# DeltaNet and multiplicative FFN on one core: the first two chunks' keys and queries transposed on TensorE, four buffers for float64 pieces, w3 and w_out loaded from ScalarE's queue, the FFN listed one chunk later

## The chip, the core and the metric

The kernel runs on one core of one Trainium2 chip. The core has five engines, each of which works through its own list of instructions in order: TensorE (PE, with its weight loads shown apart as PEld), VectorE (DVE), ScalarE (ACT), GpSimd (POOL) and SyncE (SP). SP only issues DMAs here; ACT can issue them as well. The metric is the device time of one execution in microseconds (us). A measurement of this kernel can tell a change of about 1% from no change.

## The reference

```python
def _attn_ref(q, k, v, beta):            # each (4, 8, 768, 48); beta (4, 8, 768)
    k_n = k / (np.linalg.norm(k, axis=-1, keepdims=True) + 1e-06)
    state = np.zeros((B, H, D, D))
    for t in range(S):
        kt, vt, bt = k_n[:, :, t], v[:, :, t], beta[:, :, t, None]
        y[:, :, t] = np.einsum('bhd,bhde->bhe', q[:, :, t], state)
        v_old = np.einsum('bhde,bhd->bhe', state, kt)
        state = state + bt[..., None] * np.einsum('bhd,bhe->bhde', kt, vt - v_old)

def _moe_ref(x, w1, w2, w3, w_out):      # x (3072, 384); w1, w2 (384, 1024)
    a = x @ w1                           # w3 (1024, 1024); w_out (1024, 384)
    b = x @ w2
    h = a * b @ w3
    return h @ w_out
```

The output of the first part, reordered to 3072 tokens by 384 features, is the input x of the second. The four FFN weights come as float64; q, k, v and beta as float32.

## The kernel before, in words

**Chunks.** The 768 tokens are cut into 12 chunks of 64. For one chunk all 4 batches and 8 heads are worked on together: r is the pair of batches, z the batch in it, and z picks the upper or lower half of the 128 partitions. Inside a chunk the recurrence is written as matrix products with a triangular inverse.

**What one chunk needs.** `load_tok` loads keys by token (tile `ktok`, three buffers) and `load_v` values (`vtok`). `load_perm` loads keys and queries once more, in 32x32 blocks, into the zero-padded tiles `kperm` and `qperm`: 16 small DMAs for each r, that is 32 for a chunk. `prep` turns them with DVE's 32x32 transposes into `KQ` (features on partitions, L201), multiplies keys with keys and queries on PE (L205, the "scores"), and writes `U` and `PT` on DVE (L212, L216). `norms(j)` computes the key norms of two chunks. `to_blocks`, `inverse` and `from_blocks` send U through DRAM (`Ud`), read it back as 32x32 blocks (`Ub`), invert 128 of them at a time with 62 short DVE instructions (L245, L250, tiles `tb` and `Vb`), and bring the result back through DRAM (`Vd`) into `TT`. `corner` fills the off-diagonal block with two groups of small matmuls (L274, L286). One `inverse` serves two chunks; the j-th one is called inverse(j) here, and chunks 2j and 2j+1 are pair j.

**The chain.** `chain(c)` carries the state: products of S with KQ, of R with TT, of X with ktok (all L314), and the output y (L356, L361), with one DVE step between each. ACT copies y into `xT` (L373); after the second chunk of a pair six small DMAs move some of its rows (`xT<-xT`, L380), and the pair's FFN can start.

**The weights.** `load_weight` brings a float64 piece into a `raw` buffer, two buffers in all, by SP. ACT (L397, L398), DVE (L400, L403) and POOL (L406) turn it into float32, and POOL's addition ends the use of the buffer. There are 8 pieces of w_out (`load_wo`), 16 of w3 (two in each of 8 `fold`s) and 12 of w1 and w2 (two in each of 6 `load_w12`, four DMAs a piece). A `fold` transposes its two w3 pieces on PE (L434), copies them on ACT (L436), and multiplies them with w_out into `w34` (L440), so that the FFN needs no separate product with w3.

**The FFN.** `ffn_units(u)` returns 12 units for pair u: 8 times `ab` (products with w1 and w2, L458, then L465 on ACT and L468 on DVE) and 4 times `o` (product with w34, L473, then a store of `osb`, L480). The tile `a` shares the `raw` buffers.

**The order.** The main program lists the work: loads, norms, prep and blocks of chunks 0 and 1, inverse(0), corner(0), ten weight units, then for each chunk its chain, the corner of the next, for even chunks the preparation of the next pair and its inverse, and some units of the list (`emit`). A scheduler then puts each engine's instructions into a fixed order by the dependencies, the buffers and its own idea of durations, so the order on an engine is not the order of the listing. The queue of each engine is then worked through as it stands.

Each fp32 matmul shows in the trace as two records, so 16 matmuls of a row in the order are 32 records in the profile.

## Time and profile before

| what | value |
|---|---|
| median of 3 runs | 841.39 us (837.6 to 845.68) |
| the profiled execution | 836.37 us |
| its span in the trace | 834.6 us |
| PE busy in the span | 649.6 us (78%) |
| DVE busy | 359.6 us (43%) |
| ACT busy | 150.5 us (18%) |
| POOL busy | 97.6 us (12%) |

The profile is of one execution. Its span runs from the first to the last instruction; 1.8 us of the execution lie outside it. A line of the page that cuts the span into 40 slices has one digit for each 20.9 us: the busy share in tenths. In a table by stage an engine's busy time stands with its number of instructions, followed by the granted TensorE clock (1.00 is full speed), the DMA engines' share and GB/s. In a timeline a row is start, duration, engine, source line, operation, output and input, and in brackets the idle time before it and what ended it. A row of waits gives the waiting engine and line, what ended the wait, the total in us, how often, and the longest.

### The profile page before, as it was taken

How to read it: one execution, taken by the hardware profiler on the slowest of the kernel's cores; microseconds unless marked ns; L12 is line 12 of the kernel's file. 1: busy time of each engine (PE TensorE's matmuls, PEld its weight loads, DVE VectorE, ACT ScalarE, POOL GpSimd, SP SyncE). 2: the span in 40 equal slices, each digit the busy share in tenths (PEclk: the TensorE clock that was granted, in tenths of full speed). 3: DMA queues.
4: the chain of work that ended last, by engine and by line, in shares of the span. 5: the costliest groups of instructions: out<-in, count | busy, mean ns of one | idle time of the engine just before them, and what ended most of it. 6: DMA issues, size and time to landing. Idle time of an engine off the chain costs nothing.

```text
span 834.6 us, 16954 instructions
## 1 busy us (share of the span) xinstructions
PE 649.6 (78%) x7116; PEld 401.2 (48%) x7116; DVE 359.6 (43%) x780; ACT 150.5 (18%) x305; POOL 97.6 (12%) x112
## 2 busy tenths in 40 slices
PE   0514666775718999799995998968989889996998
PEld 0502465553204656545654456553465644554444
DVE  2569453696322341862667116672166721200110
ACT  0123122233233210112201112011120021201100
POOL 4142101232321000100002001010010000000000
PEclk9756675987857989899998899997999979996999
DMA  8565326535455133432433413334112120000001
GB/s 137 101 154 125 68 39 145 131 101 128 115 120 80 22 50 75 84 68 31 68 83 88 65 17 59 77 76 84 30 30 53 49 61 1 2 29 21 0 0 38
DMA packets 218412, 56.41 MB, mean 68 GB/s; under 512 B 208544, under 2 KB 211616, under 8 KB 218336
## 3 DMA queue, kind: packets, MB, share of 16 engines
q1 hardware_dynamic: 205120, 53.52, 30.9%
q10 hardware_dynamic: 13216, 1.80, 1.4%
q8 instruction: 56, 0.92, 0.5%
q14 instruction: 20, 0.16, 0.1%
HBM read 43.09 MB, written 11.01 MB: 65 GB/s over the span
## 4 chain that ended last, share of the span: by engine, by line
PE 57%; DVE 13%; DMA 10%; SPq 5%; POOL 3%; issue 3%; ACT 2%; POOLq 0%; DVEq 0%; ACTq 0%
PE ps_f L458 27%; PE ps_f L473 15%; PE ps_w L314 6%; DVE tb L245 3%; DMA raw<-in_moe_w_dram 3%; DVE Vb L250 3%; PE ps_w L205 3%; DMA ktok<-in_k_dram 2%; PE ps_t L274 2%; POOL w L406 2%; PE ps_f L440 2%; SPq L139 1%; DMA xT<-xT 1%; DMA kperm<-in_k_dram 1%; PE ps_t L286 1%
## 5 line engine op out<-in xcount | busy, mean ns | idle before, releaser
L458 PE MATMUL ps_f<-xT,w1s 128*128 128x512 f32 x288 | 152.7, 665 | 27.7 <-DMA xT<-xT 25.8
L458 PE MATMUL ps_f<-xT,w2s 128*128 128x512 f32 x288 | 137.7, 610 | 26.2 <-ACT a L465 18.7
L473 PE MATMUL ps_f<-w,ab 128*128 128x384 f32 x384 | 125.1, 487 | 0.0
L468 DVE TENSOR_TENSOR ab<-a,ps_f 128x512 f32<-128x512 f32 x48 | 32.9, 686 | 204.9 <-PE ps_f L458 202.9
L458 PEld LDWEIGHTS ps_f<-xT,w1s 128*128 128x128 f32 x288 | 58.0, 209 | 97.5 <-issue 92.3
L458 PEld LDWEIGHTS ps_f<-xT,w2s 128*128 128x128 f32 x288 | 55.7, 197 | 98.2 <-issue 67.7
L205 PE MATMUL ps_w<-KQ 48*64 48x128 f32 x768 | 59.6, 321 | 50.1 <-DVE KQ L201 32.5
L473 PEld LDWEIGHTS ps_f<-w,ab 128*128 128x128 f32 x384 | 72.9, 190 | 52.0 <-issue 3.0
L205 PEld LDWEIGHTS ps_w<-KQ 48*64 48x64 f32 x768 | 55.0, 164 | 56.1 <-issue 33.6
L245 DVE TENSOR_TENSOR tb<-Vb,Ub 128x31 f32<-128x31 f32 (+15 forms) x186 | 73.3, 394 | 17.4 <-DMA Ub<-Ud 12.3
L250 DVE TENSOR_TENSOR Vb<-Vb,tb 128x31 f32<-128x31 f32 (+15 forms) x186 | 71.2, 383 | 5.2
L465 ACT COPY a<-ps_f 128x512 f32<-128x512 f32 x48 | 28.1, 585 | 249.1 <-PE ps_f L458 241.2
L434 PE MATMUL ps_f<-ident,w 128*128 128x128 f32 x64 | 13.8, 355 | 53.6 <-POOL w L406 53.6
L440 PE MATMUL ps_f<-wo,w3T 128*128 128x384 f32 x128 | 52.5, 573 | 0.0
L156 POOL TENSOR_TENSOR sq<-ktok 128x384 f32<-128x384 f32 x24 | 20.7, 863 | 199.4 <-DMA ktok<-in_k_dram 190.0
L303 POOL TENSOR_TENSOR vtok<-vtok,n 128x384 f32<-128x384 f32 x24 | 21.1, 884 | 188.3 <-DMA vtok<-in_v_dram 114.8
L373 ACT COPY xT<-ps_w 48x256 f32<-48x256 f32 x96 | 30.5, 365 | 68.9 <-PE ps_w L361 68.4
L440 PEld LDWEIGHTS ps_f<-wo,w3T 128*128 128x128 f32 x128 | 29.1, 234 | 20.0 <-issue 9.4
L434 PEld LDWEIGHTS ps_f<-ident,w 128*128 128x128 f32 x64 | 9.6, 179 | 57.9 <-POOL w L406 56.1
L478 ACT COPY osb<-ps_f 128x384 f32<-128x384 f32 x24 | 11.5, 478 | 129.6 <-PE ps_f L473 124.9
L406 POOL TENSOR_TENSOR w<-w,raw 128x512 uint32<-128x512 uint32 x16 | 20.8, 1300 | 76.4 <-DVE w L403 42.4
L314 PE MATMUL ps_w<-S,KQ 48*64 48x48 f32 x704 | 26.0, 234 | 3.8 <-DVE S L346 3.8
(75 smaller groups left out, 593.3 us busy)
## 6 DMA issues: line engine op xcount, KB each, us to landing
raw<-in_moe_w_dram SPq DMA_DIRECT2D x16, 512.0 KB, 4.2
vtok<-in_v_dram SPq DMA_DIRECT2D x48, 96.0 KB, 3.0
raw<-in_moe_w_dram SPq DMA_DIRECT2D x24, 192.0 KB, 3.6
out_dram<-osb SPq DMA_DIRECT2D x24, 192.0 KB, 1.9
ktok<-in_k_dram SPq DMA_DIRECT2D x40, 96.0 KB, 3.1
raw<-in_moe_w_out_dram SPq DMA_DIRECT2D x8, 384.0 KB, 3.5
Ub<-Ud SPq DMA_DIRECT2D x6, 512.0 KB, 3.3
Vd<-Vb SPq DMA_DIRECT2D x6, 512.0 KB, 2.9
```

Of the source, the lines that this page charges most:

```text
L205: nc.tensor.matmul(ps[half(z), h // 4, 128 * (h % 4) : 128 * (h % 4) + 128], lhsT=KQ[feat(z), h, 0, :], rhs=KQ[feat(z), h].rearrange("p j ...
L245: nc.vector.tensor_tensor(out=tv, in0=V[:, 0 : s + 1, s : s + 1].to_broadcast([P, s + 1, n]), in1=U[:, s, s + 1 : BS].unsqueeze(1).to_broa ...
L250: nc.vector.tensor_tensor(out=o, in0=o, in1=tv, op=ALU.subtract)
L314: nc.tensor.matmul(o, lhsT=lhs(r, h, z), rhs=rhs(r, h, z), start=True, stop=True)
L373: nc.scalar.copy(out=xT[f, :, 2 * r + z, cc, :], in_=pyv[f, z, r])
L406: nc.gpsimd.tensor_tensor(out=au, in0=au, in1=lo, op=ALU.add)
L434: nc.tensor.transpose(ps[:, x, :], w3[:, x * P : (x + 1) * P], ident[:])
L440: nc.tensor.matmul(po, lhsT=w3T[kc // 4][:, kc % 4 * P : kc % 4 * P + P], rhs=wo[kc][:, 0:DM], start=(kc == 0), stop=(kc == KF - 1))
L458: nc.tensor.matmul(ps[:], lhsT=w[:, m, js], rhs=cur["x"][:, m].rearrange("p b c t -> p (b c t)"), start=(m == 0), stop=(m == KM - 1),)
L465: nc.scalar.copy(out=a[:], in_=pair[0][:])
L468: nc.vector.tensor_tensor(out=t[:], in0=a[:], in1=pair[1][:], op=ALU.mult)
L473: nc.tensor.matmul(ps[:, 0:DM], lhsT=cur["ab"][jc][:, b * P : (b + 1) * P], rhs=w34[:, jc, :], start=(jc == 0), stop=(jc == KF - 1),)
```

## The change

There are four edits.

1. Keys and queries of chunks 0 and 1 are no longer loaded in blocks and turned by DVE. The queries are loaded by token, like the keys, into the buffers of tag X, and `by_tensor` turns both on PE against the identity (L204 of the new file), eight groups of 16 matmuls in all, with the results copied to `KQ` half by DVE and half by ACT (L213, L211). From chunk 2 on `by_vector` does what `prep` did. The padded tiles `kperm` and `qperm` are cleared later in the listing.
2. `raw` has four buffers instead of two (the tile `a` shares them).
3. The pieces of w_out and w3 are loaded by ACT's queue; w1 and w2 stay on SP. The first keys, beta and the blocks of chunks 0 and 1 move from ACT's queue to SP's; the first queries are on ACT's.
4. All w_out pieces and four folds are listed ahead of inverse(0), the other four folds right behind corner(0), and w1 and w2 after chain(0). The FFN units of a pair are appended after the `emit` of the odd chunk instead of before it, so they are listed one chunk later.

```diff
-    kperms = padded("kperm", [P, H, 2, BS], 2)
-    qperms = padded("qperm", [P, H, 2, BS], 2)
     TTs = padded("TT", [P, NR, H, C], 2)
+    kperms, qperms = [], []
...
+    def by_vector(m, r):
+        KQ = new_KQ(m, r)
+        for i, src in enumerate((kperms[r], qperms[r])):
+            nc.vector.transpose(out=KQ[:, :, i, :], in_=src[:].rearrange("p h b d -> p h (b d)"))
+
+    def by_tensor(m, r, qtok):
+        KQ = new_KQ(m, r)
+        for i, src in enumerate((ktoks[m], qtok)):
+            ps = psF.tile([P, H, C], FP32, tag="f", name="ps_f")
+            for h in range(H):
+                for z in range(2):
+                    nc.tensor.matmul(
+                        ps[feat(z), h, :], lhsT=src[half(z), r, h, :], rhs=ident[half(z), half(z)],
+                        start=True, stop=True,
+                    )
+            for z in range(2):
+                f = feat(z)
+                if z:
+                    nc.scalar.copy(out=KQ[f, :, i, :], in_=ps[f])
+                else:
+                    nc.vector.tensor_copy(out=KQ[f, :, i, :], in_=ps[f])
+
+    def scores(m, transposed):
...
-            for i, src in enumerate((kperms[r], qperms[r])):
-                nc.vector.transpose(out=KQ[:, :, i, :], in_=src[:].rearrange("p h b d -> p h (b d)"))
+            transposed(m, r)
+            KQ = KQs[m, r]
...
-    def load_weight(dst, srcs):
+    def load_weight(dst, srcs, dma):
         n = dst.shape[1]
-        raw = ffn.tile([P, CW, 2], U32, tag="raw", name="raw", bufs=2)
+        raw = ffn.tile([P, CW, 2], U32, tag="raw", name="raw", bufs=4)
         for rows, src in srcs:
-            nc.sync.dma_start(
+            dma(
...
-        load_weight(wo[j][:, 0:DM], [(slice(0, P), moe_w_out[j * P : (j + 1) * P, :])])
+        load_weight(wo[j][:, 0:DM], [(slice(0, P), moe_w_out[j * P : (j + 1) * P, :])], nc.scalar.dma_start)
...
-            load_weight(w[:, m, n0 : n0 + CW], srcs)
+            load_weight(w[:, m, n0 : n0 + CW], srcs, nc.sync.dma_start)
...
-            load_weight(w3[:], [(slice(0, P), moe_w3[rows, hf * CW : (hf + 1) * CW])])
+            load_weight(w3[:], [(slice(0, P), moe_w3[rows, hf * CW : (hf + 1) * CW])], nc.scalar.dma_start)
...
-            a = ffn.tile([P, NT], FP32, tag="raw", name="a", bufs=2)
+            a = ffn.tile([P, NT], FP32, tag="raw", name="a", bufs=4)
...
     sp, act = nc.sync.dma_start, nc.scalar.dma_start
-    load_tok(0, act)
-    load_perm(0, 0, sp)
-    load_perm(0, 1, act)
-    load_tok(1, act)
     beta_fm = ffn.tile([2 * H, NCH, 2, C], FP32, tag="xT", name="beta_fm", bufs=2)
+    load_k(0, sp)
+    q0 = load_tok(q, 0, act, "X", 2)
+    load_k(1, sp)
+    q1 = load_tok(q, 1, act, "X", 2)
...
-    prep(0)
-    to_blocks(0, act)
-    for r in range(NR):
-        load_perm(1, r, sp)
-    prep(1)
-    to_blocks(1, act)
+    for m, qt in ((0, q0), (1, q1)):
+        scores(m, lambda m, r: by_tensor(m, r, qt))
+        to_blocks(m, sp)
+    for j in range(KF):
+        load_wo(j)
+    for jc in range(KF // 2):
+        fold(jc)
     load_v(0, sp)
     inverse(0, sp)
     from_blocks(0, sp)
     corner(0)
-    units = [lambda j=j: load_wo(j) for j in range(KF)]
-    units += [lambda jc=jc: fold(jc) for jc in range(KF)]
-    units += [lambda m=m, n0=n0: load_w12(m, n0) for n0 in range(0, DF, CW) for m in range(KM)]
+    for jc in range(KF // 2, KF):
+        fold(jc)
+    kperms += padded("kperm", [P, H, 2, BS], 2)
+    qperms += padded("qperm", [P, H, 2, BS], 2)
+    units = [lambda m=m, n0=n0: load_w12(m, n0) for n0 in range(0, DF, CW) for m in range(KM)]
...
-    emit(10)
...
             inverse(c // 2 + 1, sp)
+        emit(6)
         if c % 2 == 1:
             units += ffn_units(c // 2)
-        emit(12 if c < 1 else 6)
     emit(len(units))
```

Three places show what becomes of it on the engines. First, the start of ACT's list: X is the tile of a chunk's queries, raw_423 and so on are the float64 pieces, wo_422 and so on the converted ones. Before:

```order
L139 DMA qperm1_98<-in_q_dram 32x8x16 x2
L493 DMA beta_fm_150<-in_beta_dram 8x12x64 x4
L397 ACT_TABLE_LOAD
L397 ACTIVATE wo_522<-raw_523 128x384
L398 ACTIVATE raw_523<-raw_523 128x384
L397 ACTIVATE wo_530<-raw_531 128x384
```

And now:

```order
L117 DMA X_106<-in_q_dram 64x8x48 x4
L117 DMA X_116<-in_q_dram 64x8x48 x4
L413 DMA raw_423<-in_moe_w_out_dram 128x768
L413 DMA raw_431<-in_moe_w_out_dram 128x768
L413 DMA raw_439<-in_moe_w_out_dram 128x768
L418 ACT_TABLE_LOAD
L418 ACTIVATE wo_422<-raw_423 128x384
L419 ACTIVATE raw_423<-raw_423 128x384
```

The block loads and beta are gone from ACT's queue, and three pieces of w_out are asked for right behind the queries.

Second, PE around chain(0), where w_586, w_868 and the like are w3 pieces being transposed, `wo,w3T` is a fold's product, T_449 and T_755 belong to corner(0), and `vtok,TT` and `X,ktok` are the first products of chain(0). Before:

```order
L434 MATMUL ps_f<-ident,w_586 128x128 x4
L434 MATMUL ps_f<-ident,w_601 128x128 x4
L440 MATMUL ps_f<-wo,w3T 128x384 x8
L434 MATMUL ps_f<-ident,w_626 128x128 x4
L434 MATMUL ps_f<-ident,w_641 128x128 x4
L440 MATMUL ps_f<-wo,w3T 128x384 x8
L274 MATMUL ps_t<-T_449,U 32x32 x32
L286 MATMUL ps_t<-TT_100,X_451 32x32 x32
L314 MATMUL ps_w<-vtok,TT_100 64x48 x32
L274 MATMUL ps_t<-T_791,U 32x32 x32
L314 MATMUL ps_w<-X,ktok 48x48 x32
```

And now:

```order
L455 MATMUL ps_f<-ident,w_868 128x128 x4
L455 MATMUL ps_f<-ident,w_883 128x128 x4
L461 MATMUL ps_f<-wo,w3T 128x384 x6
L295 MATMUL ps_t<-T_755,U 32x32 x32
L461 MATMUL ps_f<-wo,w3T 128x384 x2
L307 MATMUL ps_t<-TT_92,X_757 32x32 x32
L455 MATMUL ps_f<-ident,w_908 128x128 x4
L335 MATMUL ps_w<-vtok,TT_92 64x48 x32
L295 MATMUL ps_t<-T_1121,U 32x32 x32
L335 MATMUL ps_w<-X,ktok 48x48
L455 MATMUL ps_f<-ident,w_923 128x128 x4
L461 MATMUL ps_f<-wo,w3T 128x384 x8
```

Two folds stood ahead of corner(0); now six do, and the last two are threaded through chain(0).

Third, PE between chunk 5 and chunk 6. PT, X is the end of chunk 5's output, S, KQ the first product of chain(6), xT_3045 and xT_3063 the input of pair 2's FFN (chunks 4 and 5), w34, ab the FFN's last product of pair 1. Before:

```order
L361 MATMUL ps_w_3630<-PT_2308,X_3591 48x64 x2
L314 MATMUL ps_w_3866<-S_3627,KQ_3218 64x48 x16
L314 MATMUL ps_w_3866<-S_3627,KQ_3240 64x48 x16
L458 MATMUL ps_f_3791<-xT_3045,w1s_105 128x512 x3
L458 MATMUL ps_f_3795<-xT_3045,w2s_106 128x512 x3
```

And now:

```order
L382 MATMUL ps_w_3648<-PT_2326,X_3609 48x64 x2
L494 MATMUL ps_f_3869<-w34_99,ab_3477 128x384
L494 MATMUL ps_f_3869<-w34_99,ab_3489 128x384
L494 MATMUL ps_f_3869<-w34_99,ab_3501 128x384
L494 MATMUL ps_f_3869<-w34_99,ab_3513 128x384
L494 MATMUL ps_f_3869<-w34_99,ab_3525 128x384
L494 MATMUL ps_f_3869<-w34_99,ab_3537 128x384
L494 MATMUL ps_f_3869<-w34_99,ab_3819 128x384
L494 MATMUL ps_f_3869<-w34_99,ab_3831 128x384
L335 MATMUL ps_w_3884<-S_3645,KQ_3236 64x48 x16
L335 MATMUL ps_w_3884<-S_3645,KQ_3258 64x48 x16
L479 MATMUL ps_f_4459<-xT_3063,w1s_97 128x512 x3
```

Pair 2's FFN still follows the first product of chain(6), as before; what is new is that eight matmuls of pair 1's FFN stand between chunk 5's output and that place.

More of the change, by code (lines that the diff above doesn't have):

```diff
@@ L118, in load_tok, with load_k @@
                 dma(
-                    out=ktoks[m][half(z), r],
-                    in_=k[2 * r + z, :, C * m : C * m + C, :].rearrange("h t d -> t h d"),
-                )
+                    out=t[half(z), r],
+                    in_=src[2 * r + z, :, C * m : C * m + C, :].rearrange("h t d -> t h d"),
+                )
+        return t
+    def load_k(m, dma):
+        ktoks[m] = load_tok(k, m, dma, "ktok", 3)
     def load_v(m, dma):
-        vtoks[m] = work.tile([P, NR, H, D], FP32, tag="vtok", name="vtok", bufs=2)
-        for r in range(NR):
-            for z in range(2):
-                dma(
-                    out=vtoks[m][half(z), r],
-                    in_=v[2 * r + z, :, C * m : C * m + C, :].rearrange("h t d -> t h d"),
-                )
+        vtoks[m] = load_tok(v, m, dma, "vtok", 2)
     def load_perm(m, r, dma):
```

17 lines of the change are left out of this document (8 added, 9 removed).

## The prediction

> **What bounds the kernel now.** I read the page's 40 slices first.
>
> ```profile
> PE   0514666775718999799995998968989889996998
> ```
>
> Up to the twelfth slice, some 250 us, TensorE is seldom over 7 tenths busy; from there on it is nearly full. A table by stage gives the numbers (stage; length; busy us of PE, PEld, DVE, ACT, POOL with counts; PE clock; DMA share; GB/s).
>
> ```profile
> 0.00:64.00 64.00, 14.07 (x140) 13.06 (x140) 30.30 (x69) 9.09 (x17) 22.81 (x36) 0.74 0.68 134
> 64.00:130.00 66.00, 38.97 (x592) 30.64 (x592) 40.28 (x93) 14.47 (x28) 8.00 (x8) 0.68 0.38 72
> 130.00:210.00 80.00, 57.19 (x549) 40.19 (x550) 52.81 (x105) 25.25 (x46) 22.53 (x21) 0.78 0.51 130
> 210.00:254.00 44.00, 16.54 (x31) 6.32 (x30) 13.00 (x22) 12.89 (x21) 13.65 (x11) 0.69 0.50 119
> 254.00:835.00 581.00, 522.81 (x5806) 311.03 (x5806) 223.23 (x492) 88.84 (x193) 30.62 (x37) 0.93 0.25 47
> ```
>
> Until 254 us PE works 127 us, and no other engine is full: a phase of waits. After it PE works 523 of 581 us: PE-bound, with 58 us of holes. The rows of PE's waits name them, three from the first phase, the last from the second.
>
> ```profile
> PE ps_f L434 <- POOL w L406: 53.6, 10, 25.4
> PE ps_w L205 <- DVE KQ L201: 30.5, 3, 22.3
> PE ps_f L458 <- ACT a L465: 18.7, 1, 18.7
> PE ps_f L458 <- DMA xT<-xT: 25.8, 6, 7.1
> ```
>
> The largest is PE waiting for converted w3. ACT's timeline shows the pace of the conversions: w_out first, w3 from 64.72, w1 and w2 from 207.60.
>
> ```profile
> 26.98 0.56 ACT L397 ACTIVATE wo<-raw 128x384 f32<-128x384 f32 x1
> 60.04 0.55 ACT L397 ACTIVATE wo<-raw 128x384 f32<-128x384 f32 x1 [1.26 <-DMA raw<-in_moe_w_out_dram]
> 64.72 0.67 ACT L397 ACTIVATE w<-raw 128x512 f32<-128x512 f32 x1 [3.68 <-DMA raw<-in_moe_w_dram]
> 70.86 0.67 ACT L397 ACTIVATE w<-raw 128x512 f32<-128x512 f32 x1
> 76.09 0.67 ACT L397 ACTIVATE w<-raw 128x512 f32<-128x512 f32 x1
> 82.94 0.67 ACT L397 ACTIVATE w<-raw 128x512 f32<-128x512 f32 x1
> 134.45 0.66 ACT L397 ACTIVATE w<-raw 128x512 f32<-128x512 f32 x1 [17.89 <-DMA raw<-in_moe_w_dram]
> 207.60 0.66 ACT L397 ACTIVATE w1s<-raw 128x512 f32<-128x512 f32 x1
> 249.78 0.68 ACT L397 ACTIVATE w1s<-raw 128x512 f32<-128x512 f32 x1 [1.09 <-DMA raw<-in_moe_w_dram]
> ```
>
> Between the fourth and the fifth w3 piece lie 51.5 us. SP's timeline shows why: behind the raw load at 74.43 stand block loads and a key load that wait for buffers, and the next raw load leaves at 129.90.
>
> ```profile
> 74.43 0.35 SPq L392 DMA_DIRECT2D raw<-in_moe_w_dram  x1
> 74.82 4.05 SPq L139 DMA_DIRECT2D kperm<-in_k_dram  x8
> ...
> 111.45 2.65 SPq L118 DMA_DIRECT2D ktok<-in_k_dram  x4
> ...
> 129.90 0.86 SPq L392 DMA_DIRECT2D raw<-in_moe_w_dram  x2
> ```
>
> The last twelve w3 pieces take (207.60 - 134.45) / 12 = 6.1 us each; w1 and w2, ten pieces from 207.60 to 249.78, 4.2 us each.
>
> **The transposes on TensorE.** Eight DVE transposes and 64 block loads of chunks 0 and 1 go; eight query loads, 128 matmuls (256 records) and eight copies each on DVE and ACT come. The nearest rows: the DVE transpose, a group of 64 small matmuls at a low and at a higher clock, the last score mask of chunk 1 (which lets inverse(0) begin), and eight loads by token on ACT's queue.
>
> ```profile
> 68.29 0.71 DVE L201 STREAM_TRANSPOSE KQ<-kperm 128x512 f32<-128x512 f32 x1 [0.26 <-DMA kperm<-in_k_dram]
> 103.19 3.65 PE L314 MATMUL ps_w<-vtok,TT 64*64 64x48 f32 x62 [0.17 <-ACT TT L292]
> 150.66 2.07 PE L314 MATMUL ps_w<-R,TT 64*64 64x48 f32 x64
> 45.41 0.68 DVE L216 TENSOR_TENSOR PT<-ps_w,smask 128x512 f32<-128x512 f32 x1
> 0.81 9.35 ACTq L118 DMA_DIRECT2D ktok<-in_k_dram  x8
> ```
>
> DVE loses 8 x 0.71 = 5.7 us and gains eight copies of about the same size: nothing. PE gains 4 x 2.07 = 8 to 4 x 3.65 = 15 us while it would wait anyway. The scores could be earlier, but DVE's new order puts w_out conversions between the copies and the masks, and ACT's copies stand behind raw loads that wait for buffers. I keep the mask of chunk 1 at about 46 us and take nothing (bounds: 10 us earlier or later).
>
> **Four buffers, ScalarE's queue and the new order.** I follow five clock times, before and after. The load's time is the page's median to landing, the inverse is shown for its second run (the new row order threads four conversions through it, not six) and for a later one, in the group of its first instruction with first and last start.
>
> ```profile
> raw<-in_moe_w_dram SPq DMA_DIRECT2D x16, 512.0 KB, 4.2
> L245 DVE TENSOR_TENSOR tb<-Vb,Ub x31: 193/374/1433, 157.0 to 197.7; 128x31 f32<-128x31 f32 x2, 128x60 f32<-128x60 f32 x2, 128x87 f32<-128x87 f32 x2, 128x112 f32<-128x112 f32 x2
> L245 DVE TENSOR_TENSOR tb<-Vb,Ub x31: 185/357/426, 636.5 to 668.6; 128x31 f32<-128x31 f32 x2, 128x60 f32<-128x60 f32 x2, 128x87 f32<-128x87 f32 x2, 128x112 f32<-128x112 f32 x2
> ```
>
> - First w3 conversion, 64.72 before. Now the queries' issue ends at about 10 us, the first w_out lands by 15. Eight w_out pieces took (60.04 - 26.98) / 7 = 4.7 us each with two buffers; with four I take half, 2.4, so the eighth is at 32; the first w3 follows a landing later, 37 (bounds 28 and 50).
> - First w1 conversion, 207.60 before. A w3 piece is bound by a loop that buffers do not shorten: conversion, PE transposes, ACT copy, next conversion. At its shortest it shows 76.09 - 70.86 = 5.2 us, on average 6.1. I take 16 x 6.1 = 98 and no hole, plus 8 us for chain(0), which is now threaded through the last folds: 37 + 98 + 8 = 143 (bounds 37 + 83 = 120, and 190 with 8.9 a piece, which is the old mean with the hole).
> - Start of inverse(1), 157.0 before. Chain(0) must end, then norms, scores of chunks 2 and 3, the blocks through DRAM and chain(1): I take 17 us behind the folds, 160 (bounds 10 and 30).
> - End of inverse(1), 197.7 before. 32 us, the length of the 636.5 to 668.6 row, as four conversions in it stand where FFN products stand there: 192 (bounds 27 and 41 us of length; the 157.0 to 197.7 row had six conversions in it).
> - FFN runs for good, 253.81 before. SP's list has the last four w1 and w2 pieces behind inverse(1)'s store: five conversions at 2.8 us, taken between 2.1 (half of 4.2, for twice the buffers) and 4.2, are 14: 206 (bounds 5 and 21 us behind the inverse). The xT transfers stand behind these loads on SP and fall in the same time.
>
> Before, part of the FFN had run by 254: of 288 records each for w1 and w2 these rows leave 276 and 282 for the time after it.
>
> ```profile
> L458 PE MATMUL ps_f<-xT,w1s 128*128 128x512 f32 x276 | 144.1, 656 | 26.4 <-DMA xT<-xT 25.8 <-DVE ab L468 0.5
> L458 PE MATMUL ps_f<-xT,w2s 128*128 128x512 f32 x282 | 133.8, 608 | 18.7 <-ACT a L465 18.7
> 567.34 5.46 PE L458 MATMUL ps_f<-xT,w1s 128*128 128x512 f32 x6 [7.13 <-DMA xT<-xT]
> 580.55 2.74 PE L458 MATMUL ps_f<-xT,w2s 128*128 128x512 f32 x6
> ```
>
> Those 18 records are 18 x 2.74 / 6 = 8 us of work, so the old start counts as 246. Gain: 246 - 206 = 40 us.
>
> [...]
>
> Each raw load on ACT from the fifth on waits for POOL's addition of the piece four earlier. Behind it in ACT's list stand the copies of `KQ`, of the transposed w3 and of corner(0); PE and, through `KQ`, inverse(0) wait for those. I priced that in the 46 us of the mask and in the 6.1 us of the loop; rival (d) is the case that it costs more. On SP the first keys, beta, values and blocks now share one queue with nothing of w3 in between, on POOL four clears of the padded tiles move behind the norms: both have room, POOL with 23 of the first 64 us busy.
>
> **The FFN one chunk later.** In PE's row order pair 2's FFN still begins right behind the first product of chain(6), so the xT waits are not moved away. But matmuls of the pair before now stand between the odd chunk's output and that place: eight between chunks 5 and 6, five at each of the two next boundaries.
>
> ```profile
> 312.54 9.19 PE L473 MATMUL ps_f<-w,ab 128*128 128x384 f32 x28
> ```
>
> At 9.19 / 28 = 0.33 us a record, two records a matmul, they cover 5.3, 3.3 and 3.3 us: 12 us of the 25.8. What is late next is corner(2u+2) behind its inverse. Before, the path was as follows from the last scores to that corner:
>
> ```profile
> 321.66 1.97 PE L205 MATMUL ps_w<-KQ 48*64 48x128 f32 x32
> 331.87 0.36 SPq L237 DMA_DIRECT2D Ub<-Ud  x1
> 374.19 1.20 PE L274 MATMUL ps_t<-T,U 32*32 32x32 f32 x64 [0.34 <-DVE T L265]
> ```
>
> From 323.6 to 374.2 that is 50.6 us. PE's new order has between the two, at the boundary of chunks 5 and 6, six groups of 64 small matmuls at 2.07 (12 us), 12 matmuls of the kind of L473 (12 x 0.66 = 8) and 35 of L458 (35 x 0.91 = 32): 52 us, and at the other three 43, 50 and 47 by the same count. With the rest of the xT wait, about 3 us, that balances the path, and I take no wait (bounds 0 to 9 us a pair for four pairs, and 14 us more gain if the xT waits vanish).
>
> **The sum.** 834.6 - 40 - 12 = 782.6 us of span, 784 with the 1.8 outside it. The profiled execution (836.37) lies 0.6% below the median of the runs (841.39), so the forecast is 784 x 1.006 = 789 us.
>
> **The rivals.** (a) The forecast, 789, its own range 772 to 808: chance 0.52. (b) The loads are early, but the chain inverse(0), chain(0), inverse(1) is what the FFN waits for. For: DVE's row order puts inverse(0) among the conversions of w3, so it ends with the seventh fold piece or later; against: six conversions inside inverse(1) left it at 41 us. At the late bounds the FFN starts at 230, the gain is 16 + 12 and the time (834.6 - 28 + 1.8) x 1.006 = 813; chance 0.16. (c) Better: the w3 loop runs at 5.2 (14 us) and the xT waits vanish (14 us): 789 - 28 = 761; chance 0.10. (d) No change: the loop stays at 8.9 us because ACT, in order, stops at each raw load until POOL frees a buffer. The start is then 16 x 2.8 = 45 us later than in (a), the gain 40 - 45 + 12 = 7, the time (834.6 - 7 + 1.8) x 1.006 = 834, or 846 without the cover of the xT waits; chance 0.08. Against it: the addition that frees the buffer is the one that PE's next transposes wait for in any case, and ACT's next copy waits for those. (e) Slower: the inverse becomes the bound of the PE phase. In SP's new order the read-back Ub stands behind stores of the FFN's output that PE finishes only within the odd chain. From a path of about 64 us on, 13 us over PE's 51, the four pairs cost the 52 us gained; at 69 us they cost 72, and the time is (784 + 72) x 1.006 = 861. Against it: the old path already has 8 us from the scores' end to Ub, and with 5 us more it is 56. Chance 0.08. (f) The move to ACT's queue saves only issue time: 24 loads at 0.35 us, the duration at 74.43, are 8 us, the conversions otherwise keep their places, and the time is (834.6 - 8 - 12 + 1.8) x 1.006 = 821. For: the data are the same and as many. Against: the 51.5 us hole. Chance 0.06.
>
> **Chances and range.** About 1% either way, 833 to 850, can't be told from no change. Faster: (a), (b), (c), (f), 0.84. Same: (d), 0.08. Slower: (e), 0.08. Leaving out (d) and (e) and a little of (c), the range is 760 to 822.
>
> **What will show it.** Right: ACT's first w3 activation near 37 us with no gap above 10 us among the sixteen; first w1 near 143; the FFN running for good near 206; the xT waits about 14 us; PE busy unchanged near 655 us. Wrong: w3 pieces 9 us apart, PE waiting for corner's DVE transpose (L286 of the new file) in each pair, or Ub more than 15 us behind the last scores.

## The result

The changed kernel takes 748.15 us (median, 744.99 to 750.34), the kernel before, measured beside it, 840.55 us (837.6 to 845.68): a ratio of 0.889 (95% interval 0.883 to 0.895). The forecast was 789 us with a range of 760 to 822: the direction was right, the gain of 92 us was nearly twice the 52 us forecast, and the time lies below the range. The profiled execution took 746.41 us, its span is 744.7 us.

The 40 slices of the changed kernel (18.6 us each) come first, PE's busy tenths above the granted clock.

```profile
PE   1777569870079999699999999999999999999998
PEclk9888869985579999799999999999999999999999
```

PE is nearly full from the thirteenth slice on, and it has a hole that was not there before, in slices 10 and 11. The table by stage (stage; length; busy us of PE, PEld, DVE, ACT, POOL with counts; PE clock; DMA share; GB/s) has the numbers.

```profile
64.00:130.00 66.00, 47.97 (x385) 30.67 (x383) 41.44 (x89) 20.06 (x34) 13.85 (x12) 0.82 0.46 108
160.00:200.00 40.00, 4.98 (x208) 4.66 (x204) 31.29 (x74) 8.90 (x19) 7.58 (x7) 0.59 0.34 82
209.45:744.70 535.25, 515.99 (x5824) 304.25 (x5824) 225.68 (x496) 88.49 (x193) 34.91 (x43) 0.98 0.28 54
```

From 209.45 us on PE works 516 of 535 us, at a clock of 0.98. Before, the stage from 254 us on had 523 of 581 us at 0.93. The waits of PE, the first up to 200 us, the other two, in the fence behind it, from 200 us on:

```profile
PE ps_f L455 <- POOL w L427: 24.5, 8, 4.8
```

```profile
PE ps_f L479 <- DMA xT<-xT: 47.5, 3, 42.7
PE ps_t L295 <- DVE T L286: 0.9, 1, 0.9
```

The wait for converted w3 is 24.5 us instead of 53.6. Of the 47.5 us for xT one wait of 42.7 us is the new hole, so the later ones sum to 4.8 us instead of 25.8. The timelines of ACT, DVE (the group of the inverse's first instruction, with first and last start), PE and SP give the five clock times of the prediction.

```profile
35.25 0.67 ACT L418 ACTIVATE w<-raw 128x512 f32<-128x512 f32 x1
109.42 0.66 ACT L418 ACTIVATE w<-raw 128x512 f32<-128x512 f32 x1
120.52 0.67 ACT L418 ACTIVATE w<-raw 128x512 f32<-128x512 f32 x1
130.78 0.67 ACT L418 ACTIVATE w<-raw 128x512 f32<-128x512 f32 x1
131.35 0.69 ACT L418 ACTIVATE w1s<-raw 128x512 f32<-128x512 f32 x1
```

```profile
L266 DVE TENSOR_TENSOR tb<-Vb,Ub x31: 193/379/1382, 162.6 to 191.1; 128x31 f32<-128x31 f32 x2, 128x60 f32<-128x60 f32 x2, 128x87 f32<-128x87 f32 x2, 128x112 f32<-128x112 f32 x2
```

```profile
192.71 0.34 SPq L273 DMA_DIRECT2D Vd<-Vb  x1
193.10 9.75 SPq L413 DMA_DIRECT2D raw<-in_moe_w_dram  x17
203.53 4.42 SPq L401 DMA_DIRECT2D xT<-xT  x6
```

```profile
209.46 4.22 PE L479 MATMUL ps_f<-xT,w1s 128*128 128x512 f32 x6 [42.75 <-DMA xT<-xT]
310.08 5.11 PE L479 MATMUL ps_f<-xT,w1s 128*128 128x512 f32 x6 [3.51 <-DMA xT<-xT]
502.83 2.81 PE L479 MATMUL ps_f<-xT,w1s 128*128 128x512 f32 x6 [1.29 <-DMA xT<-xT]
```

| | before | forecast | after |
|---|---|---|---|
| first w3 conversion | 64.72 | 37 | 35.25 |
| first w1 conversion | 207.60 | 143 | 131.35 |
| inverse(1), first instruction | 157.0 | 160 | 162.6 |
| inverse(1), last one of the group | 197.7 | 192 | 191.1 |
| FFN runs for good | 253.81, counted as 246 | 206 | 209.46 |

Sixteen w3 pieces follow each other at (130.78 - 35.25) / 15 = 6.4 us, and the longest gap is 11.1 us (109.42 to 120.52) instead of 51.5, a little over the 10 us that the prediction allowed. So the start gained 246 - 209.46 = 36.5 us, close to the 40 forecast. The rest, 588.6 us before (834.6 - 246) and 535.2 us now (744.7 - 209.46), gained 53.4 us where 12 were forecast. That is the term that was wrong.

### The profile page after: what moved, and what is told of

Same layout as the page of the kernel before. It is cut to its first block, busy times and chain, and to the rows that moved or that the text cites. A ratio compares the mean times of both kernels' runs of the same rounds, so it can differ in the third digit from the quotient of the medians.

```text
span 744.7 us, 17392 instructions
## 1 busy us (share of the span) xinstructions
PE 631.4 (85%) x7372; PEld 391.6 (53%) x7372; DVE 356.1 (48%) x780; ACT 154.7 (21%) x313; POOL 96.1 (13%) x112
## 4 chain that ended last, share of the span: by engine, by line
PE 69%; DVE 12%; DMA 10%; issue 4%; POOL 2%; SPq 2%; ACT 1%; DVEq 0%; POOLq 0%; ACTq 0%
PE ps_f L479 31%; PE ps_f L494 16%; PE ps_w L335 8%; PE ps_w L226 5%; DVE tb L266 4%; DVE Vb L271 4%; PE ps_f L461 3%; DMA raw<-in_moe_w_dram 3%; DMA raw<-in_moe_w_out_dram 2%; PE ps_t L307 2%; PE ps_t L295 2%; POOL w L427 2%; DMA ktok<-in_k_dram 1%; PE ps_w L382 1%; PE ps_w L377 1%
## 5 line engine op out<-in xcount | busy, mean ns | idle before, releaser
L479 PE MATMUL ps_f<-xT,w1s 128*128 128x512 f32 x288 | 139.1, 614 | 50.2 <-DMA xT<-xT 47.5
L479 PE MATMUL ps_f<-xT,w2s 128*128 128x512 f32 x288 | 135.3, 599 | 0.0
L494 PE MATMUL ps_f<-w,ab 128*128 128x384 f32 x384 | 128.3, 490 | 0.0
L479 PEld LDWEIGHTS ps_f<-xT,w1s 128*128 128x128 f32 x288 | 54.2, 195 | 114.6 <-issue 63.4
L479 PEld LDWEIGHTS ps_f<-xT,w2s 128*128 128x128 f32 x288 | 53.3, 190 | 62.0 <-issue 61.4
L486 ACT COPY a<-ps_f 128x512 f32<-128x512 f32 x48 | 28.1, 585 | 207.4 <-PE ps_f L479 197.8
L226 PE MATMUL ps_w<-KQ 48*64 48x128 f32 x768 | 54.8, 296 | 6.0 <-DVE KQ L213 4.8
L226 PEld LDWEIGHTS ps_w<-KQ 48*64 48x64 f32 x768 | 48.8, 148 | 15.4 <-issue 6.3
L233 DVE TENSOR_TENSOR U<-ps_w,w 128x512 f32<-128x512 f32 x24 | 16.5, 689 | 57.6 <-PE ps_w L226 57.4
L455 PE MATMUL ps_f<-ident,w 128*128 128x128 f32 x64 | 12.5, 328 | 24.6 <-POOL w L427 24.5
L335 PEld LDWEIGHTS ps_w<-R,TT 64*64 64x64 f32 x704 | 23.6, 141 | 12.4 <-issue 6.1
L367 DVE TENSOR_TENSOR S<-S,ps_w 48x768 f32<-48x768 f32 x20 | 19.0, 952 | 22.5 <-PE ps_w L335 22.4
```

Of the source, the lines that this page charges most:

```text
L226: nc.tensor.matmul(ps[half(z), h // 4, 128 * (h % 4) : 128 * (h % 4) + 128], lhsT=KQ[feat(z), h, 0, :], rhs=KQ[feat(z), h].rearrange("p j ...
L335: nc.tensor.matmul(o, lhsT=lhs(r, h, z), rhs=rhs(r, h, z), start=True, stop=True)
L479: nc.tensor.matmul(ps[:], lhsT=w[:, m, js], rhs=cur["x"][:, m].rearrange("p b c t -> p (b c t)"), start=(m == 0), stop=(m == KM - 1),)
L486: nc.scalar.copy(out=a[:], in_=pair[0][:])
L494: nc.tensor.matmul(ps[:, 0:DM], lhsT=cur["ab"][jc][:, b * P : (b + 1) * P], rhs=w34[:, jc, :], start=(jc == 0), stop=(jc == KF - 1),)
```

## Experiments

The theory after this comparison: the 53 us come from the FFN being listed one chunk later, and most of it is not the xT wait. One rival is that the four buffers for `a`, which shares the `raw` buffers, loosened the FFN; another that the phase is only a by-product of the earlier start. The kernel before, measured beside the runs, had medians from 837.7 to 844.3 us, so differences of less than some 6 us between runs of different groups are not read.

### The FFN's place in the listing, undone and alone

```diff
-        emit(6)
         if c % 2 == 1:
             units += ffn_units(c // 2)
+        emit(6)
```

> The changed kernel with one edit undone: the FFN's units are listed before the chunk's six units are taken, as in the kernel before, so that an FFN starts behind its own odd chunk. Theory T (the unforeseen gain of the PE phase is the later FFN: its matmuls cover the xT waits and the waits between the chain's products): the phase from the FFN's start loses about 40 to 53 us, time 790 to 802, xT waits of the phase near 20 us again (4.8 in the changed kernel), clock of the phase near 0.93. Rival R1 (four a buffers instead of two loosened the FFN): only the predicted 12 us come back, time near 760. Rival R2 (a by-product of the earlier start): time 748 to 755.

The second run makes the opposite edit to the kernel before, and nothing else of the change.

```diff
         if c % 2 == 1:
             units += ffn_units(c // 2)
-        emit(12 if c < 1 else 6)
```

(with `emit(12 if c < 1 else 6)` ahead of the `if` instead)

> The kernel before with this one edit alone: the FFN's units are listed after the chunk's units are taken. T: the start is as before (FFN for good near 254), the phase behind it gains 40 to 53 us, time 788 to 800. R1 (a buffers): 12 us of gain, time near 829. R2 (by-product of the start): no gain, time near 841.

Undone: 792.39 us, ratio to before 0.941 (0.934 to 0.948), 44 us more than the changed kernel. Alone: 786.94 us, 0.933 (0.926 to 0.940), 55 us less than the kernel before. Both lie where the theory put them or a little beyond; 760 and 829 (the `a` buffers), 748 and 841 (a by-product) are out. In the second run `a` has its two buffers as before.

The first run starts the FFN at 209.16 us, so it shows the phase by itself. In a fence each: its stage from there, its xT waits (from 200 us on), its products with w1 over the whole span, and the changed kernel's row for the same products:

```profile
209.45:790.00 580.55, 531.42 (x5824) 314.89 (x5823) 223.57 (x495) 88.38 (x192) 35.44 (x43) 0.94 0.26 50
```

```profile
PE ps_f L479 <- DMA xT<-xT: 65.6, 6, 42.4
```

```profile
L479 PE MATMUL ps_f<-xT,w1s 128*128 128x512 f32 x288 | 150.2, 657 | 65.6 <-DMA xT<-xT 65.6
```

```profile
L479 PE MATMUL ps_f<-xT,w1s 128*128 128x512 f32 x288 | 139.1, 614 | 50.2 <-DMA xT<-xT 47.5 <-DVE ab L489 2.1 <-issue 0.5
```

The 45.3 us between the two spans (790.0 - 744.7) divide into three. The xT waits behind the first hole shrink from 65.6 - 42.4 = 23.2 to 4.8 us: 18.4. All idle time of the phase shrinks from 580.55 - 531.42 = 49.1 to 535.25 - 515.99 = 19.3, so other waits give 29.8 - 18.4 = 11.4; in the rows of waits, those of the chain's products for R, X and S shrink from 9.6 to 0.9 us, which is 8.7 of it. And the same 5824 records keep PE busy for 531.4 or 516.0 us: 15.4, at a granted clock of 0.94 or 0.98. Of this, 10.1 us lie in the first six records of the last five FFNs, 26.5 us in all with the FFN early and 16.3 in the changed kernel.

The second run has the whole of it without any edit of the start. This is its stage from the time when its FFN runs for good, 258.7 us:

```profile
258.70:785.90 527.20, 507.67 (x5806) 299.38 (x5806) 223.61 (x492) 89.01 (x193) 30.33 (x37) 0.99 0.27 52
```

The kernel before has the same 5806 records in its stage from 254 us on, 580.6 us to the end of its span with PE 522.8 us busy. So the one edit takes 53.4 us off the phase: the xT waits, 25.8 us, are gone, other idle time shrinks by 12.5 (57.8 to 19.5 in all), and the busy time by 15.1. One boundary, taken from the first run, shows all three. First PE in the run with the FFN early, from chunk 9's product with R to the FFN of the pair:

```profile
616.88 2.07 PE L335 MATMUL ps_w<-R,TT 64*64 64x48 f32 x64 [1.06 <-DVE R L346]
619.71 1.60 PE L335 MATMUL ps_w<-X,ktok 64*48 64x48 f32 x61 [0.77 <-DVE X L352]
...
624.95 2.07 PE L335 MATMUL ps_w<-S,KQ 48*64 48x48 f32 x64 [0.23 <-DVE S L367]
631.76 4.61 PE L479 MATMUL ps_f<-xT,w1s 128*128 128x512 f32 x6 [4.75 <-DMA xT<-xT]
```

Then the same boundary of the changed kernel:

```profile
581.10 2.02 PE L335 MATMUL ps_w<-S,KQ 48*64 48x48 f32 x64
583.05 1.56 PE L494 MATMUL ps_f<-w,ab 128*128 128x384 f32 x4
584.54 2.07 PE L335 MATMUL ps_w<-R,TT 64*64 64x48 f32 x64
586.54 1.56 PE L494 MATMUL ps_f<-w,ab 128*128 128x384 f32 x4
588.02 1.59 PE L335 MATMUL ps_w<-X,ktok 64*48 64x48 f32 x61
...
592.62 3.49 PE L494 MATMUL ps_f<-w,ab 128*128 128x384 f32 x10
596.05 2.07 PE L335 MATMUL ps_w<-S,KQ 48*64 48x48 f32 x64
598.64 2.81 PE L479 MATMUL ps_f<-xT,w1s 128*128 128x512 f32 x6 [0.52 <-issue]
```

Four records of the other pair's FFN (1.56 us) stand in the place of the 1.06 us wait for R, four in that of the 0.77 us for X, ten (3.49 us) ahead of the xT wait, and the first six FFN records, with no wait for xT ahead of them, take 2.81 instead of 4.61 us. The work between had been there before too; it had stood in front of the chain, in one piece.

### Is the slow clock caused by the waits?

```diff
+                ps = psF.tile([P, NT], FP32, tag="f", name="ps_f")
+                for m in range(2):
+                    nc.tensor.matmul(
+                        ps[:], lhsT=w1s[0:D, m, 0:P],
+                        rhs=cur["x"][0:D, m].rearrange("p b c t -> p (b c t)"),
+                        start=True, stop=True,
+                    )
```

This stands at the head of each FFN, in the kernel of the first run; the two products are work beyond the reference, and nothing reads them.

> The kernel of the first run (the changed kernel with the FFN listed early), with two matmuls more ahead of each FFN, whose result is not used: they read rows 0 to 47 of xT, which ScalarE's copies have written, and not the rows that the transfers fill, so they run inside the wait for the transfers. Theory K (about a third of the later FFN's gain, 15 of 45 us, is TensorE at a lower granted clock in and behind the waits): the wait as recorded shrinks from 4.7 to 1 to 3 us a boundary, and the first six records of an FFN take nearer to 2.74 than 5.46; over five boundaries 5 to 12 us less, time 780 to 787 against 792.4. Rival (the clock behind the waits has another cause, say the chain's small matmuls): the first six records stay at 5.46 us, and the four records more of each boundary are lost where they outlast the transfers, time 792 to 800.

Measured: 789.15 us, ratio 0.941 (0.935 to 0.946), against 0.941 for the kernel without them: no difference. At four of the five boundaries a wait for the transfers was left, 1.90 to 3.52 us long, and the first six records of the five FFNs took 5.32, 4.24, 4.92, 4.21 and 5.46 us, 24.2 in all against 26.5 without the fill. Two boundaries (the fill is L476, the FFN L486):

```profile
521.67 1.98 PE L476 MATMUL ps_f<-xT,w1s 48*128 48x512 f32 x4
526.82 4.92 PE L486 MATMUL ps_f<-xT,w1s 128*128 128x512 f32 x6 [3.17 <-DMA xT<-xT]
...
715.98 1.98 PE L476 MATMUL ps_f<-xT,w1s 48*128 48x512 f32 x4 [2.03 <-ACT xT L394]
719.86 5.46 PE L486 MATMUL ps_f<-xT,w1s 128*128 128x512 f32 x6 [1.90 <-DMA xT<-xT]
```

The fill moved the waits apart, it did not remove them: at the second boundary PE waits 2.03 us, works 1.98 and waits 1.90, and the six records behind take 5.46 us all the same. So the expected 5 to 12 us did not come, and the run does not show that the waits are what lowers the clock. It does not take the rival out either: the records stayed slow, at two boundaries as slow as the rival had them. At the first of its boundaries the fill covered the wait in full, and the fill (3.78 us) and the six records behind it (5.32) were slow all the same. So the wait right ahead of the FFN is not the whole cause; what lowers the clock is not settled.

### The edits of the start, each undone

The four kernels are the changed one with one edit undone: w_out and w3 on SyncE's queue; w_out and the folds as units behind corner(0); the first two chunks' blocks loaded and turned by DVE; two raw buffers.

```diff
-    load_weight(wo[j][:, 0:DM], [...], nc.scalar.dma_start)
+    load_weight(wo[j][:, 0:DM], [...], nc.sync.dma_start)
...
-            load_weight(w3[:], [...], nc.scalar.dma_start)
+            load_weight(w3[:], [...], nc.sync.dma_start)
```

> The changed kernel with the loads of w_out and w3 issued by SyncE again, all else as changed. Theory (SyncE's in-order list made the 51.5 us hole of the kernel before): from the eighth w3 load on they stand behind block loads of chunk 2 that wait for buffers and behind the store of inverse(0); a gap of over 20 us between w3 conversions comes back, the first w1 conversion is later than 145 (131.35 in the changed kernel), time 758 to 773. [...]

```diff
-    for j in range(KF):
-        load_wo(j)
-    for jc in range(KF // 2):
-        fold(jc)
...
-    for jc in range(KF // 2, KF):
-        fold(jc)
...
+    units = [lambda j=j: load_wo(j) for j in range(KF)]
+    units += [lambda jc=jc: fold(jc) for jc in range(KF)]
+    units += [lambda m=m, n0=n0: load_w12(m, n0) for n0 in range(0, DF, CW) for m in range(KM)]
...
+    emit(10)
...
-        emit(6)
+        emit(12 if c < 1 else 6)
```

> The changed kernel with w_out and the folds listed behind chain preparation again, as units, as in the kernel before. Theory: the first w3 pieces keep their place on ScalarE, the FFN starts within 10 us of 209, time 745 to 760. Rival (this order, not the queue, carries the start's gain): w1 conversions behind inverse(1) again, time 775 to 790.

```diff
-    q0 = load_tok(q, 0, act, "X", 2)
+    load_perm(0, 0, sp)
+    load_perm(0, 1, act)
...
-    for m, qt in ((0, q0), (1, q1)):
-        scores(m, lambda m, r: by_tensor(m, r, qt))
-        to_blocks(m, sp)
+    scores(0, by_vector)
+    to_blocks(0, sp)
+    for r in range(NR):
+        load_perm(1, r, sp)
+    scores(1, by_vector)
+    to_blocks(1, sp)
```

> The changed kernel with the first two chunks' keys and queries loaded in 32 by 32 blocks and transposed on DVE again (64 block loads, the queries' loads by token and 128 matmuls go). Theory (the edit is priced at nothing): time 745 to 755; inverse(0) within 5 us of 62 to 100. Rival (the 64 block loads crowd SyncE's and ScalarE's queues ahead of w_out, and the first w3 conversion moves from 35 to 50 or later): time 758 to 770.

```diff
-        raw = ffn.tile([P, CW, 2], U32, tag="raw", name="raw", bufs=4)
+        raw = ffn.tile([P, CW, 2], U32, tag="raw", name="raw", bufs=2)
...
-            a = ffn.tile([P, NT], FP32, tag="raw", name="a", bufs=4)
+            a = ffn.tile([P, NT], FP32, tag="raw", name="a", bufs=2)
```

> The changed kernel with two instead of four buffers for raw pieces (and for a, which shares them). Theory: w_out takes 4.7 us a piece instead of 2.4 and is done 18 us later, w3 keeps its pace of some 6.4; behind inverse(1)'s store stand two pieces more (2 x 2.8 = 6 us); FFN starts 6 to 24 us later, time 754 to 772. Rival R1 (the four a buffers are what loosens the FFN): the phase from the FFN's start loses over 20 us, time over 780. Rival (w_out and w3 are hidden behind inverse(1) in any case): 748 to 754.

| undone | time, us | ratio to before | Ub of inverse(1) read back at | Vd stored at | FFN starts at |
|---|---|---|---|---|---|
| nothing | 748.15 | 0.889 (0.883 to 0.895) | 154.50 | 192.71 | 209.46 |
| ScalarE's queue | 777.46 | 0.929 (0.925 to 0.932) | 170.81 | 211.15 | 232.58 |
| folds listed early | 754.72 | 0.901 (0.898 to 0.905) | 151.75 | 194.79 | 215.88 |
| transposes on TensorE | 779.30 | 0.931 (0.926 to 0.936) | 177.98 | 218.28 | 239.27 |
| four buffers | 766.10 | 0.915 (0.911 to 0.919) | 167.69 | 211.04 | 234.98 |

The differences are 29, 7, 31 and 18 us; the 7 are hardly more than the 6 us that can be read. Their sum, 85 us, is more than all four bring together: 39 us between the kernel with the FFN's edit alone (786.94) and the changed one, or 49 between the kernel before (841.8) and the one with all four and the FFN early (792.39). So they can't be added up. The table points to one path for three of them. There inverse(1) starts later, the FFN, which stands behind its store on SP, starts 23 to 30 us later, and the whole kernel takes 18 to 31 us more. In the fourth, the folds, inverse(1) does not start later and the FFN starts 6 us later. The stretch from the FFN's start to the end is 531 to 543 us in all four, 535 in the changed kernel. What an edit costs when it is undone need not be its gain in the kernel before, since the rest of the listing is another.

With w3 back on SP the loss of 29 us is far beyond the 8 us of rival (f), 24 loads at 0.35 us, and even above the 10 to 25 expected, but the place expected was wrong: no gap of 20 us opened among the w3 conversions. ACT's conversions and, in the second fence, SP's entries in that run:

```profile
132.85 0.68 ACT L418 ACTIVATE w<-raw 128x512 f32<-128x512 f32 x1
165.83 0.66 ACT L418 ACTIVATE w1s<-raw 128x512 f32<-128x512 f32 x1 [19.00 <-DMA raw<-in_moe_w_dram]
```

```profile
156.67 3.90 SPq L136 DMA_DIRECT2D qperm<-in_q_dram  x8
160.68 2.25 SPq L413 DMA_DIRECT2D raw<-in_moe_w_dram  x5
167.35 1.93 SPq L251 DMA_DIRECT2D Ud<-U  x4
169.33 0.95 SPq L413 DMA_DIRECT2D raw<-in_moe_w_dram  x2
170.81 0.35 SPq L258 DMA_DIRECT2D Ub<-Ud  x1
```

The last w3 piece is as early as in the changed kernel (132.85 and 130.78). Late are the entries that now stand behind w3 on SP: chunk 2's and 3's block loads, up to 160 us (113.8 in the changed kernel), then the store of their scores, 167.35, and the first w1 conversion, 165.83 instead of 131.35. Before the change w3 stood behind the block loads; here the block loads stand behind w3.

The transposes were priced at nothing, and the expected 745 to 755 us were missed by 24 to 34. Without them PE waits for the first chunks' KQ (up to 260 us; L227 and L197 are that run's lines for the scores and the DVE transposes):

```profile
PE ps_w L227 <- DVE KQ L197: 31.4, 4, 25.1
```

SP is busy with the block loads of chunk 1 until 59.20 us, where it had issued them by 37.53 before the change, and DVE's transposes now stand between conversions of the early weights. Which of the two counts more was not tried. The store of chunk 1's scores moves from 46.59 to 66.90 us, and the read-back of inverse(0) from 51.72 to 70.92, where 5 us at most were expected; inverse(1) follows. The rival there, a late start of w3, is out as well: its first conversion stood at 30.83 us. With the folds listed late the theory held (754.72 us; the FFN at 215.88). With two buffers the time fell into the expected 754 to 772, though the FFN started 25.5 us later, a little past the 6 to 24 expected. From its start to the end this kernel takes 531.2 us, no more than the changed one, so the `a` buffers are out here too.

### The new hole

Five runs with edits of the changed kernel ask why PE stands from 167 to 209 us.

```diff
-                    nc.sync.dma_start(out=xT[g : g + 16, j], in_=xT[s : s + 16, NP - 1])
+                    nc.scalar.dma_start(out=xT[g : g + 16, j], in_=xT[s : s + 16, NP - 1])
```

> The changed kernel, the six xT transfers issued by ScalarE behind its own copies instead of by SyncE. Theory Q (the 42.75 us hole before 209.46 is SyncE's order: the transfers stand behind the store that waits for inverse(1) and behind 17 loads of w1 and w2): the first FFN matmuls start near 175, but only the first half of w1 and w2 is loaded by then (four of eight column blocks, 4 x 6 matmuls at 0.5 = 12 us); time 748 - 12 = 736. Rival (PE could not use the time, because chain(2) behind inverse(1) sets the end): 748, no change.

```diff
-            load_weight(w[:, m, n0 : n0 + CW], srcs, nc.sync.dma_start)
+            load_weight(w[:, m, n0 : n0 + CW], srcs, nc.scalar.dma_start)
```

(on top of the xT transfers on ScalarE)

> As the run with the xT transfers on ScalarE, and the loads of w1 and w2 on ScalarE too, so that nothing that the FFN needs stands behind inverse(1)'s store on SyncE. Theory Q: the hole goes, FFN for good from about 178, time 748 - 30 = 718 (710 to 728). Rival (the conversions of w1 and w2 are held by DVE, which is 31 of 40 us busy between 160 and 200, and by ScalarE's loads that wait for buffers ahead of its copies): FFN from 195 or later, time 735 to 748.

xT alone: 746.31 us, no difference to 748.15, where 736 was expected. With the weights too: 758.56 us (0.901; 0.893 to 0.908), 10 us slower, where 718 was expected. Two rows of the first run and, in the fence behind them, one of the second say why.

```profile
171.80 3.75 PE L479 MATMUL ps_f<-xT,w1s 128*128 128x512 f32 x4 [5.97 <-DMA xT<-xT]
207.44 4.84 PE L479 MATMUL ps_f<-xT,w2s 128*128 128x512 f32 x6 [16.26 <-ACT a L486]
```

```profile
PE ps_t L295 <- DVE T L286: 43.6, 1, 43.6
```

In the first the FFN does start at 171.80, as expected, at a granted clock of 0.67 in the stage from 160 to 200 us, and then stops, since ACT's copy of `a` stands behind conversions of weights that SP has yet to load. PE works 13 us more in that stage and gains nothing in the end. Some 4 us of the 13 are the slow price: the 18 records ahead of the stop take 12.6 us, and 18 at 2.74 for six are 8.2. Behind the restart PE is then busy for 53.9 of the 60 us from 240 to 300 us, at a clock of 0.89, where it was busy for 59.1 at 1.00 in the changed kernel; 4.4 us of that is a new wait for `KQ` of the next scores. The rival's time came, 748, but the last run below shows that PE can use an earlier start.

In the second the scheduler put corner(2) ahead of the FFN in PE's row, and corner(2) waits 43.6 us for inverse(1). But the FFN could hardly have started earlier there: ACT's own list holds its input back, as that run's rival had it. ACT's copies of y into `xT` stand behind loads of w1 and w2 that wait for buffers, the last of which leaves at 214.00 us:

```profile
214.36 2.32 ACT L394 COPY xT<-ps_w 48x256 f32<-48x256 f32 x7 [2.45 <-DMA TT<-Vd]
```

(The bracket names what ended last by the profile; the copies need only y.) In the changed kernel these copies run at 162.82. Freeing the transfers from SP is not enough; neither the transfers nor the weights may stand behind what waits.

```diff
     for c in range(NCH):
...
+        if c == 0:
+            emit(6)
         if c % 2 == 0 and c + 2 < NCH:
             ahead(c // 2 + 1)
```

> The changed kernel with one listing moved: the six units that load w1 and w2 come after chain(0) and corner(1), ahead of the preparation of chunks 2 and 3 and of inverse(1), instead of behind it; the xT transfers then stand ahead of inverse(1)'s store on SyncE. Theory Q2 (the 42.75 us hole needs both, the weights and xT free of inverse(1); with xT alone PE stopped again at 191 for the weights): FFN starts near 185 and PE then has some 27 FFN products (25 us) ahead of corner(2); inverse(1) moves 10 us later by the conversions put ahead of it; time 725 to 738. Rival (the inverse of each pair is by now the pace of the whole kernel, so every us that inverse(1) moves later is paid at the end): 755 to 760.

> The same, with the xT transfers issued by ScalarE. Theory Q2: within 5 us of the run with the listing alone, since SyncE has nothing that waits ahead of them there any more. Rival (SyncE's other entries still hold the transfers): 8 us or more faster than that run.

Here the units of w1 and w2 are listed ahead of inverse(1): 739.47 us (0.879; 0.872 to 0.886), and 736.81 us with xT on ScalarE as well (0.874; 0.865 to 0.883), the two alike as expected. Both are faster than the changed kernel, by 9 and 11 us, though the first one's interval (0.872 to 0.886) overlaps the changed kernel's (0.883 to 0.895). The first misses 725 to 738 narrowly: its FFN starts at 205.58 us and not near 185, and inverse(1) moved further than the 10 us assumed, its Ub read back at 193.50 instead of 154.50 us; PE waited 33.6 us for the scores ahead of it. That a kernel with inverse(1) 39 us later is no slower also takes the rival out that the inverses set the pace of all that follows.

```diff
-            load_weight(w[:, m, n0 : n0 + CW], srcs, nc.sync.dma_start)
+            load_weight(w[:, m, n0 : n0 + CW], srcs, nc.gpsimd.dma_start)
```

(with xT on ScalarE, the listing as in the change)

> The changed kernel with w1 and w2 loaded by GpSimd and the xT transfers issued by ScalarE, the listing as changed: the weights' loads stand behind nothing of inverse(1) but the buffers. Theory Q2: FFN starts near 175 and PE has some 18 FFN products ahead of corner(2), inverse(1) in its old place: time 730 to 740. Rival (48 loads issued by GpSimd delay its additions, on which the conversions wait): 748 or more.

This one takes 728.16 us (727.63 to 730.97), ratio 0.866 (0.859 to 0.873), 2.7% below the changed kernel and a little under the 730 to 740 expected: the fastest of all. Its first FFN records and, in the second fence, PE's largest wait from 130 us on:

```profile
177.04 5.11 PE L479 MATMUL ps_f<-xT,w1s 128*128 128x512 f32 x6 [6.99 <-DMA xT<-xT]
```

```profile
PE ps_f L479 <- ACT a L486: 10.1, 1, 10.1
```

The FFN starts 32 us earlier, and the hole of 42.7 us is down to waits of 7 and 10 us and, ahead of corner(2), one of 3.7. The 48 loads did not delay POOL's additions for w3: its last conversion stands at 130.66 us, 130.78 in the changed kernel.

## Why the prediction was wrong, and where it was right

**The start held.** All five clock times came within 12 us and the one that counts, the FFN's start, within 4. The pieces of w3 kept to their loop (6.4 us instead of 6.1), and the first w1 conversion was 12 us early for no gain, since the FFN stood behind inverse(1).

**The step that failed** is "they cover 5.3, 3.3 and 3.3 us: 12 us of the 25.8". It priced the later FFN at 12 us; undoing that edit alone cost 45.3 us of span, and making it alone in the kernel before took 53.4 us off the phase. Three things were missing from it. It counted three boundaries and left out the last: there half an FFN now stands between chunk 11 and the last pair's FFN, where the early listing waits 5.9 us; with it the 12 become 18, and 18.4 were measured. At the three counted boundaries the waits shrink by 3.7, 3.5 and 4.8 us, 11.9 in all, and not by 5.3, 3.3 and 3.3: that the sum fits so well is luck. It looked at the xT wait alone and not at the other waits, above all those for R, X and S inside the odd chunk's chain, which the same few matmuls cover: 11.4 us, 8.7 of them for R, X and S. And it took PE's work as fixed, "PE busy unchanged near 655 us", while its own two rows, 5.46 us for six records behind a wait and 2.74 us without, showed the same work at two prices: 15.4 us. The remaining 8 us of the phase's 53.4 are idle time that is gone already in the run with the FFN early (57.6 us before, 588.6 less 531; 49.1 there), so the other edits take them when the FFN is early. With the FFN late alone they are gone as well; the two gains overlap.

**The transposes at nothing.** The mask stayed at about 46 us, as the prediction said: chunk 1's scores were stored at 46.59. But beside the other edits the single edit is worth something: without it that store comes at 66.90 us, and the kernel takes 31 us more. For the sum it did not matter, since all edits were made; as a price of the single edit it was wrong.

**The rivals.** (b) named the right path, inverse(0), chain(0), inverse(1), and in three of the four runs with an edit of the start undone the FFN's start moves with inverse(1); but in the changed kernel it starts at about the forecast's time and not at 230 us. (c), with 14 us for vanished xT waits, pointed the right way and was too small. (d) fell with the 6.4 us a piece. (e) fell with the 0.9 us that PE waits for corner's DVE transpose. (f) fell with w3 back on SyncE's queue: 29 us, not 8. That the move saves only the time to issue, no run shows. The w3 conversions kept their pace there, as (f) would have it (the last at 132.85 us, 130.78 in the changed kernel), but SP's block loads, scores and loads of w1 came late, since they stood behind w3 in its list (the first w1 conversion at 165.83 us instead of 131.35).

## What to carry to other kernels

Where a serial chain and an independent block share an engine, list the block one stage later, so that pieces of it are left to stand between the chain's steps: a few matmuls per wait (1.56 us for waits of 0.8 to 1.1) did it here, and they were work that had to be done anyway. Where TensorE waits, read the records around the wait as well as the wait: here 29.8 us less waiting came with 15.4 us less busy time for the same 5824 records, at a granted clock of 0.98 instead of 0.94. And do not add up edits that act on one path: four edits of the start cost 7 to 31 us each when undone, 85 in sum, and were together worth 39 to 49.

## What the runs showed of the hardware

The granted clock fell to 0.50 near waits of a few us. In the changed kernel six FFN records take 5.11 us behind a wait of 3.51 us, at a granted clock of 0.55, and 2.81 us behind one of 1.29 us, at 1.00 (310.08 and 502.83). But the longer wait is not what lowered the clock: it begins at 306.57, and the clock was down before. Two stages of one us and, behind them, PE's row in that time:

```profile
303.00:304.00 1.00, 0.88 (x46) 0.89 (x47) 0.86 (x3) 0.13 (x1) 0.55 (x1) 1.00 0.02 5
305.00:306.00 1.00, 1.00 (x24) 1.00 (x23) 0.00 (x0) 0.96 (x4) 0.00 (x0) 0.50 0.00 0
```

```profile
303.60 2.97 PE L335 MATMUL ps_w<-S,KQ 48*64 48x48 f32 x62
```

From 305 us on the clock is 0.50, while PE is fully busy and this product takes 2.97 us, where 64 records of its kind take 2.07 at other boundaries; its longest wait in the ten us before is 1.56 us, ahead of 303.12. The kernel before shows the same: a clock of 0.50 from 348 us on, ahead of a wait of 3.00 us and six records at 5.46 (351.76). In both the clock is 1.00 again while the FFN runs, from 315 and from 358 us on. So the wait ahead of the FFN is not what lowered it, and no run here shows what did.

The kernel with the fill has another such case, at 715.98 and 719.86: 2.03 us of wait, 1.98 of matmuls on 48 rows and 1.90 of wait were followed by six records at 5.46 us. The four records of the fill were not slow there: 1.98 us, where they take 3.78 at the first boundary. So 1.98 us of work between the two waits did not keep the six records at the 2.74 us that six take from 727.94 us on. What would have, no run here shows.
